# A block-sparse attention and feed-forward kernel on one core: block table by two VectorE operations, opening loads reordered, issue times of the DMA queue in the scheduler

## The chip, the core and the metric

The kernel runs on one NeuronCore of a Trainium2 chip. The metric is the device time of one execution in microseconds (us), the median of several. The engines are TensorE (PE in the profile; PEld is its weight load), VectorE (DVE), ScalarE (ACT), GpSimd (POOL) and SyncE (SP), which here only issues transfers. A DMA can be issued by SP, ACT or POOL, each with its own queue.

Runs more than 1.5% above the fastest of the same kernel count as slow; ratios use fast runs alone. A span (first to last instruction) is a little shorter than the time of the same run (275.8 and 277.58 us in the profiled run of the changed kernel).

## The reference, cut to what matters

```python
q, k, v: (4, 8, 768, 64)   sampled_blocks: (24, 3)   w_in: (512, 2048)   w_out: (2048, 512)
mask = |blk_i - blk_j| <= 1, or first/last block row or column, or kb in sampled_blocks[qb]   # blocks of 32
attn = softmax(where(mask, q @ k.T / 8, -1e9)) @ v
x    = attn.transpose(0, 2, 1, 3).reshape(4 * 768, 512)
out  = relu(x @ w_in) ** 2 @ w_out
```

## The kernel before

Heads go in pairs: `u` is a head pair, 0 to 3 in the first image, 4 to 15 in the other three. Scores are made transposed (keys by queries), go through one exponential per tile on ACT (`pT`), are multiplied on DVE by a table of the mask (`MK`), and meet the values on PE. The result, normalized (`xq`), is transposed (`xT`) by PE in the first image and by a transposing DMA in the others, and goes through the two layers (`ph` is the hidden one, `py` the output). PE must do all matmuls, so the kernel is built to keep PE fed.

The first 256 queries need the mask before `MK` exists. They get it by an extra matmul of a block table `oh` (128x768, one where a key lies in a block) with mask rows `R`. `oh` was cut out by GpSimd, and copied to the other half by DVE:

```python
V.memset(oh, 1.0)
G.affine_select(out=o3, in_=o3, compare_op=AOP.is_ge, fill=0.0, base=0, ...)
G.affine_select(out=o3, in_=o3, compare_op=AOP.is_ge, fill=0.0, base=block - 1, ...)
V.tensor_copy(out=oh[D:P, :], in_=oh[0:D, :])
```

The loads of the opening are a list: queue, head pair, which of queries 0, keys 1, values 2, and which part. Rows are 1536 bytes for a whole load, 768 for half of the keys, 512 for the first two of six query chunks:

```python
sy.dma_start(out=sb_i, in_=sampled_blocks.bitcast(I32))
for eng, u, w, ns in ((sc_, 0, 1, KEYS[0]), (sy, 0, 0, QRS[0]), (sc_, 1, 1, ALL), (sy, 0, 1, KEYS[1]),
                      (sy, 1, 0, QRS[0]), (sy, 0, 2, ALL), (sc_, 1, 2, ALL), (sy, 2, 1, ALL),
                      (sy, 2, 0, QRS[0]), ...
```

Everything after that is placed by a list scheduler in the program itself. It keeps a modelled clock per engine, takes the task that can start first (or an urgent one), and so fixes the order in which each engine gets its instructions. It never sees the chip: it works from numbers such as these.

```python
LAT = {"PE": 0.23, "DVE": 0.06, "ACT": 0.06, "POOL": 0.08, "SP": 2.0}
LEAD = 13.709                                 # how far ahead casts of later keys may start
arrive = {(0, 1, 0): 4.15, (0, 0, 0): 4.7, (0, 1, CP): 6.4, (0, 2, 0): 8.8, (1, 1, 0): 7.0, ...   # opening loads
ld_t = T_(("SP", 1.3), s0 - 30, load, u, (sy, sy, sy), ..., dma=3.3)             # loads of u >= 4
mu[u, q0] = T_(("SP", 0.5), s - 9, x_transp_dma, u, q0, w, deps=[nm], ..., dma=0.4)
```

The softmax here doesn't subtract the row's maximum and nothing guards it: scores larger than these inputs give would overflow.

## Time and profile before

| | before |
|---|---|
| time, median of 3 | 280.29 us (279.68 to 281.26) |
| span of the profiled run | 279.2 us |
| PE / ACT / DVE / POOL busy | 96% / 73% / 70% / 38% |
| PE waits for `xT` | once, 3.0 us, near 104 us |

How to read it: PE is the bound, so each microsecond is either PE's work or PE's lost time. The stretches of the profile show where it is lost. Columns are the window, its length, busy time and count of PE, weight load, DVE, ACT and POOL, then the granted clock, the DMA share and GB/s.

```profile
0.00:31.00 31.00, 27.50 (x468) 20.82 (x470) 24.63 (x71) 21.42 (x32) 14.62 (x33) 1.00 1.05 248
...
101.00:109.00 8.00, 4.97 (x38) 2.40 (x33) 2.96 (x7) 3.27 (x6) 2.01 (x3) 0.79 1.04 219
```

PE lacks 3.5 of 31 us in the opening and 3.0 of 8 us where the second image's hidden layer starts. In that second stretch the clock too falls to a mean of 0.79. In the opening, the timeline (start, duration, engine, line, operation, out<-in, and in brackets the idle time before it and what ended it) shows what the first tiles hang on.

```profile
1.79 0.51 ACTq L221 DMA_DIRECT2D vs<-in_v_dram  x1
...
6.37 0.23 PE L386 MATMUL ps<-QK 64*128 64x128 bf16 x2
...
7.01 0.81 ACT L397 ACTIVATE pT<-ps 128x768 bf16<-128x768 f32 x1 [1.57 <-PE ps L390]
7.17 1.02 DVE L195 CAST qc<-ks 128x384 bf16<-128x384 f32 x2 [0.71 <-DMA ks<-in_k_dram]
...
7.78 0.34 PE L338 MATMUL pt<-identb,qc 128*128 128x128 bf16 x3 [0.81 <-DVE qc L195]
```

The first score tile starts at 6.37, its exponential at 7.01, and the second half of the first keys is cast at 7.17. ACT's queue takes 384 KB of values (pair 1) at 1.79 us, among the first loads.

### The profile page before, as it was taken

Reading aid. Unit: us, or ns where it says so; the run is one execution under the profiler, and the core shown is the slowest. Engines: PE = TensorE matmul, PEld = TensorE weight load, DVE = VectorE, ACT = ScalarE, POOL = GpSimd, SP = SyncE. Lnnn points to the kernel's source line nnn. Section 1 sums busy time; section 2 is a strip of 40 time slices with the busy share of each in tenths; the row PEclk is TensorE's granted clock in tenths of the full one; section 3 lists DMA queues with packets and bytes.
Section 4 is the critical chain, followed back from the end, with each engine's and each line's share of the span. In section 5 each row is a group of like instructions: output and inputs, shape, how many; then the busy total and the mean of one; then the engine's idle time right before and its main releaser. Section 6 shows DMA issues by size and latency. Waiting matters only on the chain.

```text
span 279.2 us, 7467 instructions
## 1 busy us (share of the span) xinstructions
PE 268.4 (96%) x3037; PEld 164.1 (59%) x3037; DVE 195.7 (70%) x394; ACT 202.4 (73%) x304; POOL 107.1 (38%) x136
## 2 busy tenths in 40 slices
PE   8889999999999969999999999999999999999995
PEld 5668767566766535566555565555555555555544
DVE  7877899899687836778867688676767774344400
ACT  3588989899999765999899798978988850011111
POOL 4462437564756314444312132111131426655500
PEclk9999999999999997999999999999999999999999
DMA  6999999999915997462033344212101111111112
GB/s 217 366 231 206 197 236 368 316 340 278 255 22 90 258 246 248 59 197 59 12 72 80 86 116 52 65 21 59 47 13 56 40 32 47 39 40 38 38 67 85
DMA packets 51882, 36.93 MB, mean 132 GB/s; under 512 B 30984, under 2 KB 48904, under 8 KB 51848
## 3 DMA queue, kind: packets, MB, share of 16 engines
q1 hardware_dynamic: 46808, 31.27, 41.5%
q0 software_dynamic: 4224, 4.19, 9.3%
q10 hardware_dynamic: 816, 0.98, 1.0%
q8 instruction: 24, 0.39, 0.6%
q14 instruction: 10, 0.08, 0.1%
HBM read 27.26 MB, written 6.29 MB: 120 GB/s over the span
## 4 chain that ended last, share of the span: by engine, by line
PE 83%; DMA 7%; DVE 6%; ACT 2%; issue 1%; SPq 1%; ACTq 0%; DVEq 0%
PE ph L473 28%; PE py L514 28%; PE po L419 13%; PE ps L386 12%; DVE pT L404 3%; DMA qs<-in_q_dram 3%; DMA vs<-in_v_dram 2%; DMA xT<-xq 2%; DVE qc L195 1%; ACT pT L397 1%; PE pk L308 1%; DVE xq L429 1%; PE po L436 1%; PE ps L390 0%; SPq L221 0%
## 5 line engine op out<-in xcount | busy, mean ns | idle before, releaser
L397 ACT ACTIVATE pT<-ps 128x1024 bf16<-128x1024 f32 (+1 forms) x148 | 140.3, 1000 | 14.2 <-PE ps L386 8.9
L491 POOL TENSOR_TENSOR g<-r 128x384 bf16<-128x384 f32 (+1 forms) x86 | 75.1, 876 | 130.5 <-DVE r L482 71.9
L473 PE MATMUL ph<-xT,w_in_sb 128*128 128x384 bf16 (+2 forms) x640 | 108.1, 296 | 3.0 <-DMA xT<-xq 3.0
L404 DVE TENSOR_TENSOR pT<-pT,MK 128x1024 bf16<-128x1024 bf16 x132 | 101.4, 784 | 10.9 <-ACT pT L397 10.5
L514 PE MATMUL py<-w_out_sb,g 128*128 128x512 bf16 (+1 forms) x400 | 102.3, 370 | 0.1
L473 PEld LDWEIGHTS <-w_in_sb 128*128 128x128 bf16 x640 | 52.8, 98 | 33.2 <-issue 4.4
L482 DVE TENSOR_SCALAR r<-ph 128x384 f32<-128x384 f32 (+1 forms) x82 | 43.1, 527 | 38.3 <-PE ph L473 30.8
L419 PEld LDWEIGHTS <-pT 128*128 128x128 bf16 x1152 | 47.3, 98 | 21.2 <-issue 5.1
L419 PE MATMUL po<-VT,pT 128*128 128x65 bf16 x1152 | 54.6, 194 | 0.4 <-DVE xT L195 0.3
L514 PEld LDWEIGHTS <-g 128*128 128x128 bf16 x400 | 36.0, 97 | 25.5 <-issue 1.5
L386 PE MATMUL ps<-QK 64*128 64x256 bf16 (+1 forms) x624 | 47.6, 263 | 0.4 <-ACT pT L397 0.2
L489 ACT ACTIVATE g<-r 128x384 bf16<-128x384 f32 (+1 forms) x58 | 28.7, 496 | 19.1 <-DVE r L482 18.3
L386 PEld LDWEIGHTS <-QK 64*128 64x128 bf16 x624 | 25.1, 94 | 22.5 <-issue 18.8
L193 ACT COPY ys<-py 128x512 f32<-128x512 f32 (+1 forms) x23 | 13.0, 567 | 31.8 <-PE py L514 31.7
L480 ACT ACTIVATE r<-ph 128x256 f32<-128x256 f32 (+1 forms) x62 | 26.3, 444 | 4.7 <-PE ph L473 3.7
L195 POOL CAST VT<-vs 128x768 bf16<-128x768 f32 x15 | 13.9, 932 | 25.2 <-PE po L419 16.5
L429 DVE TENSOR_TENSOR xq<-po,rs 128x256 bf16<-128x256 f32 (+1 forms) x52 | 21.0, 404 | 1.8
L427 DVE RECIPROCAL rs<-po 128x4 f32<-128x4 f32 (+1 forms) x52 | 9.1, 175 | 13.6 <-PE po L419 13.4
L195 DVE CAST qc<-qs 128x768 bf16<-128x768 f32 (+2 forms) x14 | 8.8, 632 | 0.9 <-DMA qs<-in_q_dram 0.9
L195 DVE CAST qc<-ks 128x768 bf16<-128x768 f32 (+1 forms) x11 | 7.8, 713 | 1.2 <-DMA ks<-in_k_dram 1.2
L390 PE MATMUL ps<-R,oh 64*128 64x128 bf16 x96 | 6.8, 216 | 0.0
L338 PE MATMUL pt<-identb,qc 128*128 128x128 bf16 x48 | 4.9, 226 | 1.8 <-DVE qc L195 1.8
(55 smaller groups left out, 74.6 us busy)
## 6 DMA issues: line engine op xcount, KB each, us to landing
out_dram<-ys SPq DMA_DIRECT2D x23, 256.0 KB, 2.0
vs<-in_v_dram SPq DMA_DIRECT2D x15, 384.0 KB, 6.0
ks<-in_k_dram SPq DMA_DIRECT2D x14, 384.0 KB, 5.1
qs<-in_q_dram SPq DMA_DIRECT2D x12, 384.0 KB, 4.2
w_in_sb<-in_moe_w_in_dram POOLq DMA_DIRECT2D x4, 512.0 KB, 9.3
w_out_sb<-in_moe_w_out_dram POOLq DMA_DIRECT2D x4, 512.0 KB, 12.1
qs<-in_q_dram SPq DMA_DIRECT2D x4, 256.0 KB, 7.1
xT<-xq SPq DMA_TRANSPOSE x36, 2.3
```

Of the source, the lines that this page charges most:

```text
L195: (V if e == "DVE" else G).tensor_copy(out=out, in_=in_)
L386: nc.tensor.matmul(ps[:, h, j * w:(j + 1) * w], QK[i][hs, 1, ksl], QK[i][hs, 0, qsl], start=j == 0, stop=not add, skip_group_check=True)
L397: A.activation(out=pT[:, :, 0:n], in_=stile.pop(a)[:, :, 0:n], func=AF.Exp, scale=scale)
L404: V.tensor_tensor(out=pT, in0=pT, in1=m[:, None].broadcast_to([P, 2, len(cs), w]), op=AOP.mult)
L419: nc.tensor.matmul(po[:, qc, h, :], pT[:, h, j * w + qc * P:j * w + (qc + 1) * P], VT[i][:, h, n, 0:VW], start=(n == 0 and qc == 0 and h = ...
L429: V.tensor_tensor(out=xq, in0=po[:, :, :, 0:D], in1=rs.broadcast_to([P, n, 2, D]), op=AOP.mult)
L473: nc.tensor.matmul(htile[T, f][:, i * w:(i + 1) * w], w_in_sb[:, kc, f_ * P:(f_ + 1) * P], xT[b][:, kc, c0:c0 + w], start=(kc == 0), stop= ...
L480: A.activation(out=r, in_=src, func=AF.Relu)
L482: V.tensor_scalar(out=r, in0=src, scalar1=0.0, scalar2=None, op0=AOP.max)
L489: A.activation(out=g, in_=r, func=AF.Square)
L491: (G if e == "POOL" else V).tensor_mul(out=g, in0=r, in1=r)
L514: nc.tensor.matmul(ytile[T, i], gtile[T, f][:, ts * P:(ts + 1) * P], w_out_sb[:, f, cs[0]:cs[1]], start=(f == 0), stop=(f == NF - 1))
```

## The change

Its intent: free GpSimd and VectorE in the opening by a cheaper block table, load in the order of need, and give the scheduler truer times for SP's DMA queue, so that loads no longer stand in front of an urgent transpose. Constants of the scheduler were tuned again around it. The core of the diff:

```diff
-    N_WARM, N_IDLE = 15, 24
+    N_WARM, N_IDLE = 14, 24
-    MASKED = ((256, 768, 17.0), (0, 256, 38.0))
+    MASKED = ((256, 512, 12.0), (512, 768, 20.0), (0, 256, 38.0))
-    LAT = {..., "SP": 2.0}
+    LAT = {..., "SP": 1.4}
-    LEAD = 13.709
+    LEAD = 9.283
...
-    sy.dma_start(out=sb_i, in_=sampled_blocks.bitcast(I32))
-    for eng, u, w, ns in ((sc_, 0, 1, KEYS[0]), (sy, 0, 0, QRS[0]), (sc_, 1, 1, ALL), (sy, 0, 1, KEYS[1]),
-                          (sy, 1, 0, QRS[0]), (sy, 0, 2, ALL), (sc_, 1, 2, ALL), (sy, 2, 1, ALL),
-                          (sy, 2, 0, QRS[0]), (sy, 3, 1, ALL), (sy, 3, 0, QRS[0]), (sy, 2, 2, ALL), (sy, 3, 2, ALL),
+    for eng, u, w, ns in ((sc_, 0, 1, KEYS[0]), (sy, 0, 0, QRS[0]), (sc_, 1, 1, ALL), (sy, None, 0, ALL), (sy, 0, 1, KEYS[1]),
+                          (sy, 1, 0, QRS[0]), (None, 0, 0, ALL), (sc_, 0, 2, ALL), (sy, 2, 1, ALL), (sy, 2, 0, QRS[0]),
+                          (sy, 3, 1, ALL), (sy, 3, 0, QRS[0]), (sy, 1, 2, ALL), (sy, 2, 2, ALL), (sy, 3, 2, ALL),
...                       # u None: the block list; eng None: the load of ACT's function table
-    V.memset(oh, 1.0)
-    G.affine_select(out=o3, ...)          # twice
-    V.tensor_copy(out=oh[D:P, :], in_=oh[0:D, :])
+    V.tensor_scalar(out=place.rearrange("a (j i) -> a j i", i=block), in0=blk[:, 0:nb, None].broadcast_to([P, nb, block]),
+                    scalar1=blk[:, nb:nb + 1], scalar2=None, op0=AOP.is_equal)
+    V.tensor_copy(out=oh.rearrange("a (n p) -> a n p", p=P), in_=place.rearrange("a (p n) -> a n p", n=NCH))
...
-    arrive = {(0, 1, 0): 4.15, (0, 0, 0): 4.7, (0, 1, CP): 6.4, (0, 2, 0): 8.8, (1, 1, 0): 7.0, (1, 0, 0): 7.4, ...
+    arrive = {(0, 1, 0): 3.7, (0, 0, 0): 3.8, (0, 1, CP): 5.0, (1, 0, 0): 5.7, (1, 1, 0): 5.8, (0, 2, 0): 7.8, ...
-            ld_t = T_(("SP", 1.3), ..., dma=3.3)
+            ld_t = T_(("SP", 1.6), ..., dma=4.0)
-                    mu[u, q0] = T_(("SP", 0.5), ..., dma=0.4, **kw)
+                    mu[u, q0] = T_(("SP", 1.22), ..., dma=0.6, **kw)
...                       # likewise the transposes of later keys and queries, the stores, the relu and
...                       # square biases (0.364, 0.372 -> 0.192, 0.21), PACE, AHEAD, TIES and the start times
```

More of the change, by code (lines that the diff above doesn't have):

```diff
@@ L77 @@
     QT0, ADDED, ALONE = [(0, 128), (128, 128), (256, 256), (512, 256)], (0, 128), (0, 128)
-    MASKED = ((256, 768, 17.0), (0, 256, 38.0))
+    MASKED = ((256, 512, 12.0), (512, 768, 20.0), (0, 256, 38.0))
     tasks = []
-    LAT = {"PE": 0.23, "DVE": 0.06, "ACT": 0.06, "POOL": 0.08, "SP": 2.0}
+    LAT = {"PE": 0.23, "DVE": 0.06, "ACT": 0.06, "POOL": 0.08, "SP": 1.4}
     OVER = {"PE": 0.0, "DVE": 0.08, "ACT": 0.09, "POOL": 0.03, "SP": 0.0}
     SWITCH, SHARE, SLACK = 0.096, 0.85, 0.1
-    AHEAD = {"PE": 0.007, "DVE": 0.022, "ACT": 0.153, "POOL": 0.0, "SP": 0.0}
-    LEAD = 13.709
-    PACE0, PACE, SINGLE, MASK_AT = 39.252, 1.548, 1, 17.0
+    AHEAD = {"PE": 0.027, "DVE": 0, "ACT": 0.139, "POOL": 0.0, "SP": 0.0}
+    LEAD = 9.283
+    PACE0, PACE, SINGLE, MASK_AT = 43.821, 1.719, 1, 17.0
     class Buf:
@@ L89, in __init__ @@
             self.pool, self.holds, self.free = pool, 0, 0.0
-    TIES = 369548, 1.681, 1.912
+    TIES = 808178, 1.778, 0.874
     def tie(n):
@@ L225 @@
     sb_i = consts.tile([nb, n_rand * 2], I32, name="sb_i")
-    sy.dma_start(out=sb_i, in_=sampled_blocks.bitcast(I32))
-    for eng, u, w, ns in ((sc_, 0, 1, KEYS[0]), (sy, 0, 0, QRS[0]), (sc_, 1, 1, ALL), (sy, 0, 1, KEYS[1]),
-                          (sy, 1, 0, QRS[0]), (sy, 0, 2, ALL), (sc_, 1, 2, ALL), (sy, 2, 1, ALL),
-                          (sy, 2, 0, QRS[0]), (sy, 3, 1, ALL), (sy, 3, 0, QRS[0]), (sy, 2, 2, ALL), (sy, 3, 2, ALL),
+    for eng, u, w, ns in ((sc_, 0, 1, KEYS[0]), (sy, 0, 0, QRS[0]), (sc_, 1, 1, ALL), (sy, None, 0, ALL), (sy, 0, 1, KEYS[1]),
+                          (sy, 1, 0, QRS[0]), (None, 0, 0, ALL), (sc_, 0, 2, ALL), (sy, 2, 1, ALL), (sy, 2, 0, QRS[0]),
+                          (sy, 3, 1, ALL), (sy, 3, 0, QRS[0]), (sy, 1, 2, ALL), (sy, 2, 2, ALL), (sy, 3, 2, ALL),
                           (sy, 0, 0, QRS[1]), (sy, 1, 0, QRS[1]), (sy, 2, 0, QRS[1]), (sy, 3, 0, QRS[1])):
-        load_part(eng, u, w, ns)
-    nc.scalar.add_instruction(mybir.InstLoadActFuncSet(
-        act_func_set_id=ACT_SET_LN_EXP, name=nc.get_next_instruction_name(),
-        engine=mybir.EngineType.Activation, ins=[], outs=[]))
+        if eng is None:
+            nc.scalar.add_instruction(mybir.InstLoadActFuncSet(
+                act_func_set_id=ACT_SET_LN_EXP, name=nc.get_next_instruction_name(),
+                engine=mybir.EngineType.Activation, ins=[], outs=[]))
+        elif u is None:
+            sy.dma_start(out=sb_i, in_=sampled_blocks.bitcast(I32))
+        else:
+            load_part(eng, u, w, ns)
     warm = consts.tile([P, 256], BF, name="warm")
@@ L241 @@
     oh = consts.tile([P, S], BF, name="oh")
-    V.memset(oh, 1.0)
     bm = consts.tile([nb, P], BF, name="bm")
     V.memset(bm, 0.0)
+    place = consts.tile([P, S], BF, name="place")
+    blk = consts.tile([P, nb + 1], F32, name="blk")
     junk = ps_h.tile([P, 512], F32, name="junk", tag="h")
@@ L250 @@
     rel = consts.tile([nb, nb], F32, name="rel")
-    col = consts.tile([nb, nb], F32, name="col")
-    row = consts.tile([nb, 1], F32, name="row")
     small = dict(allow_small_or_imprecise_dtypes=True)
+    G.iota(blk[:, 0:nb], pattern=[[1, nb]], base=0, channel_multiplier=0, **small)
+    for h in range(2):
+        G.iota(blk[h * D:(h + 1) * D, nb:nb + 1], pattern=[[0, 1]], base=0, channel_multiplier=1, **small)
     G.iota(rel, pattern=[[1, nb]], base=0, channel_multiplier=-1, **small)
-    G.iota(col, pattern=[[1, nb]], base=0, channel_multiplier=0, **small)
-    G.iota(row, pattern=[[0, 1]], base=0, channel_multiplier=1, **small)
+    col, row = blk[0:nb, 0:nb], blk[0:nb, nb:nb + 1]
     identb = consts.tile([P, P], BF, name="identb")
     make_identity(nc, identb)
-    o3 = oh.rearrange("a (n p) -> a n p", p=P)
-    G.affine_select(out=o3, in_=o3, compare_op=AOP.is_ge, fill=0.0, base=0,
-                    pattern=[[1, NCH], [NCH, P]], channel_multiplier=-block)
-    G.affine_select(out=o3, in_=o3, compare_op=AOP.is_ge, fill=0.0, base=block - 1,
-                    pattern=[[-1, NCH], [-NCH, P]], channel_multiplier=block)
     QK, VT = [], []
@@ L528, in T_ @@
         return Task(engs, key, (lambda e: f(*args, e)), **kw)
-    arrive = {(0, 1, 0): 4.15, (0, 0, 0): 4.7, (0, 1, CP): 6.4, (0, 2, 0): 8.8, (1, 1, 0): 7.0, (1, 0, 0): 7.4, (1, 2, 0): 9.1,
-              (2, 1, 0): 9.8, (2, 0, 0): 9.9, (3, 1, 0): 11.4, (3, 0, 0): 11.7, (2, 2, 0): 12.8, (3, 2, 0): 13.8}
-    arrive.update({(u, 0, 2): (14.6, 16.2, 16.6, 17.3)[u] for u in range(HP)})
+    arrive = {(0, 1, 0): 3.7, (0, 0, 0): 3.8, (0, 1, CP): 5.0, (1, 0, 0): 5.7, (1, 1, 0): 5.8, (0, 2, 0): 7.8, (2, 1, 0): 7.9, (2, 0, 0): 8.3,
+              (3, 1, 0): 9.4, (3, 0, 0): 9.8, (1, 2, 0): 10.8, (2, 2, 0): 11.9, (3, 2, 0): 12.95}
+    arrive.update({(u, 0, 2): (14.9, 15.4, 16.1, 16.8)[u] for u in range(HP)})
     KEYS_OF = {P: [tuple(range(CP)), tuple(range(CP, NCH))], QW: [(2 * c, 2 * c + 1) for c in range(CP)]}
@@ L554, in prepare @@
             g = gate[GATES[min(u - HP, len(GATES) - 1)]]
-            ld_t = T_(("SP", 1.3), s0 - 30, load, u, (sy, sy, sy),
-                      deps=cv[u - NRAW] + tr[u - NRAW] + [g], dma=3.3)
+            ld_t = T_(("SP", 1.6), s0 - 30, load, u, (sy, sy, sy),
+                      deps=cv[u - NRAW] + tr[u - NRAW] + [g], dma=4.0)
             at = dict(deps=[ld_t])
@@ L562, in prepare @@
                 tr[u].append(c)
-                x = T_(("SP", 1.0), s0 - 10, transp_dma, u, w, deps=[c] + old_s, put=[qc], dma=1.2)
+                x = T_(("SP", 1.25), s0 - 10, transp_dma, u, w, deps=[c] + old_s, put=[qc], dma=1.5)
                 ev[u].update({(w, n): x for n in range(NCH)})
@@ L575, in prepare @@
                 opts["ACT"] = 0.23 + 0.1 * n
-                if u or (w == 0 and ns.start):
+                if u or w == 0:
                     opts["POOL"] = 0.1 + 0.15 * n
@@ L588, in prepare @@
             for i in range(2 * NWP):
-                wl[i] = T_(("POOL", 0.85), -50 + i, w_load, i, after=12.9 + 2.55 * i - (1.7 if i else 0), late=1.3, dma=2.55)
+                wl[i] = T_(("POOL", 0.85), -50 + i, w_load, i, after=11.9 + 2.6 * i - (1.7 if i else 0), late=1.3, dma=2.62)
             for i in GATES:
@@ L613, in attend @@
                 ob[u, q0] = Buf("po")
-            va = T_(("PE", 0.245 * part), s + 2.929, values, a, deps=[ex] + cv[u] + va_all[-1:],
+            va = T_(("PE", 0.245 * part), s + 2.393, values, a, deps=[ex] + cv[u] + va_all[-1:],
                     get=[] if cs[0] else [ob[u, q0]], put=[pt], mode=128)
@@ L627, in attend @@
                 if by_dma:
-                    mu[u, q0] = T_(("SP", 0.5), s - 9, x_transp_dma, u, q0, w, deps=[nm], put=[xqb], dma=0.4, **kw)
+                    mu[u, q0] = T_(("SP", 1.22), s - 9, x_transp_dma, u, q0, w, deps=[nm], put=[xqb], dma=0.6, **kw)
                     continue
@@ L639 @@
         rb_ = Buf("ps")
-        t = T_(("PE", 0.11 + 0.11 * i), -90 + i, mask_rows, c0, c1, after=9.5 if i else 5.5, get=[rb_], put=[], mode=32)
-        mr.append(T_({"ACT": 0.4 + 0.2 * i, "DVE": 0.3 + 0.2 * i}, -88 + i, mask_rows_evac, c0, c1, deps=[t], put=[rb_], after=10.0 if i else 0.0))
+        t = T_(("PE", 0.11 + 0.11 * i), -90 + i, mask_rows, c0, c1, after=8.5 if i else 4.15, get=[rb_], put=[], mode=32)
+        mr.append(T_({"ACT": 0.4 + 0.2 * i, "DVE": 0.42 + 0.25 * i}, -88 + i, mask_rows_evac, c0, c1, deps=[t], put=[rb_], after=8.5 if i else 0.0))
     for i in range(N_IDLE):
@@ L693 @@
                         put=[xb[b]] if last_use else [], mode=128)
-                rr = T_(RELU[w], 200, relu, t, f, deps=[h1], get=[rb], put=[hb], bias={"ACT": 0.364})
-                sq = T_(SQ[w], n_key, square, t, f, deps=[rr], get=[gb], put=[rb], bias={"ACT": 0.372})
+                rr = T_(RELU[w], 200, relu, t, f, deps=[h1], get=[rb], put=[hb], bias={"ACT": 0.192})
+                sq = T_(SQ[w], n_key, square, t, f, deps=[rr], get=[gb], put=[rb], bias={"ACT": 0.21})
                 sq_of.update({(t, f + i): sq for i in range(per_unit(t))})
@@ L711 @@
                     yc = T_({"ACT": 0.22 + 0.365 * n, "DVE": 0.15 + 0.53 * n}, 150, out_copy, t, i, cs, deps=[yy], get=[sb], put=[yb])
-                    T_(("SP", 0.2), 0, store, t, i, ts, cs, deps=[yc], put=[sb], late=2.0)
-    run_schedule({"PE": 4.65, "DVE": 5.3, "ACT": 4.15, "POOL": 4.4, "SP": 16.0},
+                    T_(("SP", 0.55), 0, store, t, i, ts, cs, deps=[yc], put=[sb], late=2.0, dma=0.7)
+    run_schedule({"PE": 4.2, "DVE": 4.0, "ACT": 3.65, "POOL": 3.7, "SP": 16.0},
                  {"ps": 2, "po": 1, "h": 2, "y": 1, "pT": PT_BUFS, "r": R_BUFS, "g": G_BUFS, "ys": YS_BUFS,
-                  "qc": QC_BUFS, "xq": XQ_BUFS, "xT": XT_BUFS}, dma_free=16.4)
+                  "qc": QC_BUFS, "xq": XQ_BUFS, "xT": XT_BUFS}, dma_free=15.4)
 _INS = ['q', 'k', 'v', 'sampled_blocks', 'moe_w_in', 'moe_w_out']
```

## The prediction

> **What bounds the kernel now.** First I read the page's busy times, to see which engine the end can hang on:
>
> ```profile
> PE 268.4 (96%) x3037; PEld 164.1 (59%) x3037; DVE 195.7 (70%) x394; ACT 202.4 (73%) x304; POOL 107.1 (38%) x136
> ```
>
> TensorE (PE) is busy for 96% of 279.2 us, so time can only come from its idle stretches and from matmuls that run slower than they must. "Busy" hides the second kind, so I made a ledger: every matmul in program order, priced at the start-to-start time that the chain of waits shows for an undisturbed run of its form (eight 256-wide hidden matmuls in 0.87 us, so 0.109 each; four 384-wide in 0.65; four 512-wide output ones in 0.86; sixteen value ones in 0.59; eight 256-wide score ones in 0.54; 128-wide score pairs 0.056 a pair). The sum is 260.6 us. Setting it against the true start of each matmul shows where the other 18.6 us go:
>
> - 1.3 before the first matmul;
> - 7.0 between there and 31 us (the opening);
> - 1.7 from 31 to 101 us;
> - 4.7 from 101 to 109 us;
> - 0.3 in the following 167 us;
> - 3.6 from the last matmul's start to the end (last copy and store).
>
> Two of these are what the change can reach. Next I asked the chain of waits about the 4.7 us; columns are start, duration, what:
>
> ```profile
> 99.57 5.36 DMA xT<-xq
> 104.97 1.78 PE ph L473 x5
> ```
>
> A transposing DMA of x, issued at 99.57, holds the first hidden matmuls of batch 1. The DMA queue's timeline shows why it came so late: its xq was written by 96.65, but the queue was first busy with three loads (0.58 + 0.46 + 0.47 us of issuing), another transpose (1.17) and a store:
>
> ```profile
> 95.99 0.58 SPq L210 DMA_DIRECT2D qs<-in_q_dram  x1
> 96.62 0.46 SPq L210 DMA_DIRECT2D ks<-in_k_dram  x1
> 97.12 0.47 SPq L210 DMA_DIRECT2D vs<-in_v_dram  x1
> 97.69 1.17 SPq L448 DMA_TRANSPOSE xT<-xq  x1
> 98.96 0.52 SPq L523 DMA_DIRECT2D out_dram<-ys  x1
> 99.57 1.19 SPq L448 DMA_TRANSPOSE xT<-xq  x1
> ```
>
> Then it took 5.36 us to land, behind those loads' 1.2 MB, where the median transpose lands in 2.3. The stretches of one microsecond show the price; columns are PE, weight load, DVE, ACT, POOL busy, then the granted clock, DMA share, GB/s:
>
> ```profile
> 103.00:104.00 1.00, 0.00 (x0) 0.00 (x0) 0.00 (x0) 0.33 (x1) 0.00 (x0) 1.00 0.86 130
> 104.00:105.00 1.00, 0.03 (x1) 0.03 (x2) 0.00 (x0) 0.00 (x0) 0.00 (x0) 0.77 1.14 279
> 105.00:106.00 1.00, 1.00 (x4) 0.50 (x5) 0.41 (x1) 0.00 (x0) 0.00 (x0) 0.50 1.14 323
> ```
>
> PE stands still for 3.03 us, and as it resumes the granted clock is 0.50 for some 3 us more: the five matmuls of the chain took 1.78 us instead of 5 x 0.162 = 0.8. Ledger: 3.2 of standing, 1.5 of half clock.
>
> Last, the opening, in the timeline:
>
> ```profile
> 2.14 0.83 DVE L277 SCALAR_TENSOR_TENSOR pm<-rel,pm 24x24 f32<-24x24 f32 x1
> 3.01 1.25 DVE L279 TENSOR_SCALAR al<-pm,edge 24x24 f32<-24x24 f32 x1
> 9.47 0.81 ACT L397 ACTIVATE pT<-ps 128x768 bf16<-128x768 f32 x1 [1.65 <-PE ps L390]
> 15.85 0.74 DVE L195 CAST qc<-qs 128x512 bf16<-128x512 f32 x1 [0.91 <-DMA qs<-in_q_dram]
> ```
>
> Two 24x24 operations take 0.83 and 1.25 us while GpSimd runs the two affine selects of the block table; bm is ready at 5.57. ACT, which must do 16 exponentials before the wide tiles start, has its second only at 9.47 because keys of head pair 0 (second half) were cast at 7.17; the late queries at 15.85 then hold PE for 1.1 us. DMA moved 362 GB/s from 5 to 8 us, so the opening is a matter of which bytes come first.
>
> **What the Trainium skill says.** "TensorE: Matmul & The Clock Gate", What's actually happening: an idle window of about 3.4 us sends TensorE to half clock and about 3.4 us of activity brings it back, the window running freely. The trace agrees (3.03 us idle, then 0.50), so a wait of 3 us costs half as much again and a wait of 0.5 us should cost itself alone. "GPSIMD Engine Reference", Specifications: GpSimd shares SBUF interfaces with VectorE, in contention with VectorE's 2-port modes and two-input operations. Agrees: 0.83 and 1.25 us beside the affine selects, 0.10 to 0.13 us for their neighbours of the same size. "DMA: Bandwidth & Descriptors", Issuing engines are not separate DMA queues: issuing on several engines saves only the sequencer's time. So moving loads between ACT's and SP's queues gains order, not bandwidth.
>
> **The change part by part.** *Block table.* Out: memset (0.70), two affine selects on POOL (0.87, 0.86), copy of half (0.35). In: one tensor_scalar and one strided copy of 128x768 on DVE. I put them at 0.4 to 0.9 us each (the memset of that shape takes 0.70), the same DVE time, but 2 us of POOL work go and the two slowed operations should shrink by about 1.8 us together. bm at about 4.4, 1.2 us earlier. POOL being free also takes the first query cast.
>
> *Loads.* The first query load is issued at once rather than behind the block list (0.50 us earlier), and the 384 KB of values of pair 1 move behind the keys of pairs 2 and 3. At 362 GB/s that is 1.1 us that all data in between come earlier. The second exponential should start near 8 us instead of 9.5, the fifth near 12 instead of 13.6; the late queries can gain no more than the 0.5 us of the earlier start. They held PE before; in the new order PE meets their transposes about 1 us of work later, so that wait should mostly go. Sum: the wide tiles (exponential 17, at 26.0 before) start about 1.5 us earlier. These gains are on the path, as PE's order is fixed and everything behind shifts.
>
> *Queue model.* No instruction changes, but the order does. I counted, in the two programs, PE work between the last value matmuls that a hidden tile needs and its first hidden matmul. For the stalled tile it is 5.41 us before and 4.15 after, so less. But in the new queue order that transpose has a store and a transpose in front, and no loads nearby. It then needs 0.7 (reciprocal 0.18, multiply 0.42, semaphores), 0.1 for the queue, and 2.3 to land, 3.1 in all: under 4.15. At the other batch changes the program leaves 4.58 us twice, and 4.55 sufficed at one of them before. So I take 4.4 of the 4.7 us as gained.
>
> *Mask table in two steps.* 18 mask matmuls of 256 instead of 6 of 512 and 6 of 256: equal columns on PE, six more evacuations, each 0.1 to 0.2 us of overhead: about 1 us spread over ACT and DVE.
>
> *Engine choice.* The lower bias sends squares to ACT: 58 to 89, and relus 62 to 72, off POOL and DVE. Back to back these cost ACT 0.26 to 0.43 us, so some 13 us more, of which 15 squares fall after the last scores where ACT idles. But between exponentials 20 and 56 my sum of ACT's work rises from 48.6 to 51 us, against PE work of 51.2: ACT is then as full as PE. I charge 0.4 us there and 0.2 later.
>
> *PE work itself*: one warm-up matmul less, 0.2.
>
> Sum: -1.5 -4.4 -0.2 +0.4 +0.2 = -5.5, at most. Some of the opening's gain will meet the weight loads, which run at full DMA rate from 14 to 37 us and begin only about 0.5 to 1 us earlier: I take back 0.4. So 280.3 - 5.1 = 275.2.
>
> **The rivals.**
> 1. *The stall stays or moves.* Only 4.15 us lie in front of the first hidden matmul, and DVE could be inside a mask product (0.68 us, up to 1.4 in this trace) when the values end. For it: the margin is one microsecond, and the last of four accumulation steps adds 0.5. Against: the freed queue. A wait of 1 us would give 276.2; the full stall with its half clock 279.8.
> 2. *ACT becomes the bound from 31 to 100 us.* For it: its sum equals PE's. If every extra microsecond of ACT's work showed up, the 2.4 us would give 277.2. Against: from exponential 80 to 92 ACT was busy 17.3 of 18.7 us and PE lost nothing.
> 3. *The opening gains nothing*, because DMA carries the same bytes and the late queries still arrive near 15.5. Then 276.7. Its opposite, all gaps of ACT before 25 us (4.7 us in sum) halved, gives 274.
>
> **Range and chances.** Removing the stall is the solid part (4 to 5 us), the opening 0.5 to 2.3, ACT's price 0 to 2. So 275.2, with 273.5 to 277.8 for 8 in 10. Faster by over 2% needs 274.7, just below my number: 0.41; within 2%: 0.58; slower by over 2% would need a new stall of twice the old one: 0.01.
>
> **What would show each step.** The chain should have no piece of several us of the x transpose near 100 us, and no stretch with PEclk below 0.9 after the warm-up; that transpose should be issued within 0.2 us of its xq and land in about 2.3. The two 24x24 operations should take under 0.3 us, bm be ready before 4.8, the second exponential start before 8.5 and the seventeenth near 24.5. ACT's idle time between 31 and 100 us should shrink without PE waiting on "pT" or "ps" for more than 2.5 us in sum. The prediction is wrong if PE shows a wait of over 1 us after 30 us, or if the seventeenth exponential starts after 25.5.

## The result, and the profile after

The changed kernel takes 277.23 us (median of 4, 276.86 to 278.12) against 280.12 for before. The ratio is 0.9895 with a 95% interval of 0.9855 to 0.9935, a gain of 1.05%. A ratio is the mean time of one kernel's fast runs over that of the other's of the same rounds, so it is not quite the ratio of the medians quoted beside it. The point prediction was 275.2; the range held, the sum did not.

The page's busy times and clock row, after (the clock in tenths, 40 slices):

```profile
PE 266.1 (96%) x3003; PEld 165.4 (60%) x3042; DVE 192.1 (70%) x389; ACT 219.4 (80%) x349; POOL 74.4 (27%) x101
...
PEclk9689999999999999999999999999999999999999
```

ACT has more to do, POOL less, as intended. (39 matmul records are missing, so x3003; all weight loads are there.) The low digits of the clock row have moved from the 16th slice to the second: out of the image change, into the opening. The stretches:

```profile
0.00:31.00 31.00, 26.85 (x433) 20.20 (x434) 21.45 (x65) 20.39 (x34) 11.77 (x31) 0.89 1.06 248
31.00:101.00 70.00, 69.06 (x931) 47.65 (x944) 58.38 (x120) 65.18 (x111) 23.93 (x31) 1.00 0.84 204
101.00:109.00 8.00, 7.95 (x88) 4.56 (x88) 6.64 (x12) 7.37 (x14) 4.63 (x6) 1.00 0.90 207
```

From 101 to 109 us PE is now busy for 7.95 of 8.00 us at full clock (4.97 and 0.79 before). In the opening it does less than before, at 0.89 of the clock. SP's queue shows how the stall went:

```profile
95.27 1.17 SPq L448 DMA_TRANSPOSE xT<-xq  x1
96.62 0.45 SPq L523 DMA_DIRECT2D out_dram<-ys  x1
98.38 1.18 SPq L448 DMA_TRANSPOSE xT<-xq  x1
```

No load stands between them. The normalized tile is written at 98.34 and its transpose is issued at 98.38, lands 2.3 us later, near 100.7, and the first hidden matmul starts at 101.67 with PE never idle.

The opening is the other half. The chain of waits of the changed kernel (start, duration, what):

```profile
2.21 6.02 DMA qs<-in_q_dram
8.25 0.83 DVE qc L195
9.13 0.40 PE pt L338 x2
```

The load of 128 KB of queries for pair 1, issued at 2.21, takes 6.02 us. The timeline beside it, with VectorE's part first:

```profile
1.29 0.73 DVE L269 TENSOR_SCALAR place<-blk 128x768 bf16<-128x768 f32 x1
2.06 0.94 DVE L271 COPY oh<-place 128x768 bf16<-128x768 bf16 x1
...
3.32 0.28 DVE L280 TENSOR_SCALAR al<-pm,edge 24x24 f32<-24x24 f32 x1
...
4.71 0.18 DVE L288 TENSOR_SCALAR bm<-pm 24x48 bf16<-24x48 f32 x1
...
6.87 0.55 DVE L195 CAST qc<-ks 128x384 bf16<-128x384 f32 x1 [1.08 <-DMA ks<-in_k_dram]
```

The block table does what it should: the 24x24 operation that took 1.25 us takes 0.28, and `bm` is ready at 4.89 instead of 5.57. But VectorE then stands idle for 1.08 us until the second half of the first keys lands. The rest of the timeline:

```profile
1.83 0.46 ACTq L221 DMA_DIRECT2D vs<-in_v_dram  x1
...
7.48 0.34 PE L338 MATMUL pt<-identb,qc 128*128 128x128 bf16 x3 [1.46 <-DVE qc L195]
...
8.30 0.81 ACT L397 ACTIVATE pT<-ps 128x768 bf16<-128x768 f32 x1
...
11.11 0.61 PE L322 MATMUL idle<-warm 128*128 128x128 bf16 x4
11.21 0.81 ACT L397 ACTIVATE pT<-ps 128x768 bf16<-128x768 f32 x1 [2.10 <-PE ps L390]
```

In this order PE meets the transposes of that key half *before* the first scores, so the first exponential starts at 8.30 instead of 7.01 and the second at 11.21 instead of 9.47. The line of `idle` matmuls is a useful clock: these keep-warm matmuls never change, and four of them in a row take 0.61 us here, at half clock, and 0.40 at full clock (shown for another run below). ACTq's line explains the load: the values of pair 0, formerly on SP's queue, are now on ACT's at 1.83, where those of pair 1 were at 1.79 before. ACT's queue carries as many bytes in the first microseconds as it did before.

The prediction's ledger can be made for every trace: the start of each weight load minus the undisturbed cost of all PE work in front of it is the time lost so far. By stage, in us ("opening" is up to 22.5 us of PE work, near 30 us; "image change" from 90 to 95 us of work, near 100; the tail runs from the last weight load to the end):

| profiled run | opening | middle | image change | later | tail | PE work | span |
|---|---|---|---|---|---|---|---|
| before | 8.07 | 1.63 | 4.81 | 0.36 | 3.8 | 260.6 | 279.2 |
| changed | 10.51 | 0.67 | 0.23 | 0.45 | 3.7 | 260.4 | 275.8 |
| changed, run again | 8.93 | 0.69 | 0.23 | 0.45 | 3.6 | 260.4 | 274.2 |

(The last matmul's own work, about 0.1 us, lies in the tail, so the sums run 0.1 over.) The stall is gone, 4.6 us. The middle gains 1.0. The opening gives 2.4 us back in one profiled run and 0.9 in another of the same kernel.

### The profile page after: what moved, and what is told of

It is laid out like the page before. It is cut to its first block, busy times and chain, and to the rows that moved or that the text cites.

```text
span 275.8 us, 7401 instructions
## 1 busy us (share of the span) xinstructions
PE 266.1 (96%) x3003; PEld 165.4 (60%) x3042; DVE 192.1 (70%) x389; ACT 219.4 (80%) x349; POOL 74.4 (27%) x101
## 4 chain that ended last, share of the span: by engine, by line
PE 88%; ACT 4%; DMA 2%; DVE 2%; issue 1%; SPq 0%; ACTq 0%
PE py L514 28%; PE ph L473 28%; PE po L419 14%; PE ps L386 13%; ACT pT L397 3%; DMA qs<-in_q_dram 2%; PE pt L338 1%; PE ps L390 1%; PE pk L308 1%; DVE pT L404 1%; PE idle L322 1%; DVE qc L195 1%; ACT r L480 1%; ACT g L489 1%; PE po L436 1%
## 5 line engine op out<-in xcount | busy, mean ns | idle before, releaser
L404 DVE TENSOR_TENSOR pT<-pT,MK 128x1024 bf16<-128x1024 bf16 x132 | 100.1, 775 | 11.9 <-ACT pT L397 11.3
L473 PE MATMUL ph<-xT,w_in_sb 128*128 128x384 bf16 (+2 forms) x640 | 105.7, 294 | 0.1
L514 PE MATMUL py<-w_out_sb,g 128*128 128x512 bf16 (+1 forms) x361 | 94.4, 370 | 1.8
L491 POOL TENSOR_TENSOR g<-r 128x384 bf16<-128x384 f32 (+1 forms) x55 | 48.6, 889 | 167.3 <-ACT r L480 87.3
L482 DVE TENSOR_SCALAR r<-ph 128x384 f32<-128x384 f32 (+1 forms) x72 | 36.7, 512 | 29.7 <-PE ph L473 28.7
L489 ACT ACTIVATE g<-r 128x384 bf16<-128x384 f32 (+1 forms) x89 | 43.2, 494 | 17.7 <-DVE r L482 17.1
L480 ACT ACTIVATE r<-ph 128x384 f32<-128x384 f32 (+1 forms) x72 | 31.9, 464 | 6.2 <-PE ph L473 5.9
L193 ACT COPY ys<-py 128x512 f32<-128x512 f32 (+1 forms) x19 | 10.7, 565 | 10.2 <-PE py L514 10.2
L195 DVE CAST qc<-ks 128x768 bf16<-128x768 f32 (+1 forms) x13 | 10.1, 774 | 1.1 <-DMA ks<-in_k_dram 1.1
L390 PE MATMUL ps<-R,oh 64*128 64x128 bf16 x96 | 7.7, 231 | 0.0
```

What stands on the lines that cost most here:

```text
L195: (V if e == "DVE" else G).tensor_copy(out=out, in_=in_)
L404: V.tensor_tensor(out=pT, in0=pT, in1=m[:, None].broadcast_to([P, 2, len(cs), w]), op=AOP.mult)
L473: nc.tensor.matmul(htile[T, f][:, i * w:(i + 1) * w], w_in_sb[:, kc, f_ * P:(f_ + 1) * P], xT[b][:, kc, c0:c0 + w], start=(kc == 0), stop= ...
L480: A.activation(out=r, in_=src, func=AF.Relu)
L482: V.tensor_scalar(out=r, in0=src, scalar1=0.0, scalar2=None, op0=AOP.max)
L489: A.activation(out=g, in_=r, func=AF.Square)
```

## The experiments

My theory after the result had two parts. First, the stall went because no loads stand in front of the transpose, whichever number of the scheduler moved them. Second, the opening got slower because PE's new order is written for loads that arrive near 5.0 and 5.7 us (the new `arrive` table), while ACT's queue still takes the bandwidth with values that nobody needs yet. Rivals: the block table is the cause, the mean clock of the opening is an accident of these runs, or the retuned order alone is slower. Twelve kernels ran; before had medians of 279.25, 279.95 and 279.92 us (11 runs each). All results were correct.

### The changed kernel again

No edit.

> The changed kernel again, beside the others of this call. Theory: 277.2 us; the first exponential near 8.3 and the second near 11.2 us, later than the 7.0 and 9.5 of the kernel before, in every run and not only in the profiled one. Rival: the slow opening belongs to that one profiled execution, whose granted clock fell to 0.5 from 8.4 to 15.3 us; then the second exponential comes before 9.5 us here and the time goes under 276.

Measured: 278.33 us (276.01 to 280.23), ratio 0.9938 [0.9886, 0.9990]; one of the six runs is slow. In the profiled run, the fastest of the six, the first two exponentials start at 8.13 and 10.45 us, late as expected; the other runs have no trace. The spread of 4 us is wider than that of any variant below in which the second exponential starts before 10 us (at most 2.4), but the kernel before, whose second starts at 9.47, spreads by 3.2 to 6.0 us over its 11 runs, so spread alone does not point to late keys. The gain over before lies between 0.6% (here) and 1.05%.

### Values of pair 0 behind the first keys and queries

```diff
-  (sy, 1, 0, QRS[0]), (None, 0, 0, ALL), (sc_, 0, 2, ALL), ...
+  (sy, 1, 0, QRS[0]), (None, 0, 0, ALL), (sy, 0, 2, ALL), ...
```

All orders on PE, DVE, ACT and POOL are those of the changed kernel; one load changes its queue.

> The changed kernel with one load moved: the values of head pair 0 go from ACT's queue to SP's, behind the first queries of pair 1. All five engines' compute orders are the same. Theory (the 384 KB on ACT's queue take turns with the keys and queries on SP's queue and delay them): the second half of the keys of pair 0 is cast before 5.8 us (6.87 now), the queries of pair 1 before 6.5 (8.25 now), the second exponential starts before 8.6 (11.21 now), the granted clock stays at 1.0 after the warm-up, and the time falls by 1.5 to 2.5 us to about 275.2. Rival (SP's small rows are slow by themselves, whatever ACT's queue does): these loads land at most 0.3 us earlier and the time stays at 277.

Measured: 274.87 us (273.57 to 275.98), ratio 0.9824 [0.9784, 0.9863], against 0.9938 for the changed kernel. The timeline:

```profile
5.66 0.55 DVE L195 CAST qc<-ks 128x384 bf16<-128x384 f32 x1
6.40 0.29 DVE L195 CAST qc<-qs 128x256 bf16<-128x256 f32 x1 [0.18 <-DMA qs<-in_q_dram]
...
8.10 0.40 PE L322 MATMUL idle<-warm 128*128 128x128 bf16 x4
8.21 0.81 ACT L397 ACTIVATE pT<-ps 128x768 bf16<-128x768 f32 x1 [0.30 <-PE ps L390]
```

The keys are cast at 5.66 (6.87 in the changed kernel), the queries at 6.40 (8.25), the second exponential starts at 8.21 (11.21), and the keep-warm matmuls run at full clock. The bytes that landed on each queue in each microsecond, counted from the transfer records, in KB:

```
us from start          2-3  3-4  4-5  5-6  6-7
changed     ACT queue   99  359  154  210   97
            SP queue   108    4  175   47  216
values late ACT queue   90  362  123    0    0
            SP queue   109    5  219  281  376
```

From 3 to 4 us nearly everything goes to ACT's queue in both (359 and 362 KB against 4 and 5). This is no sharing yet: by the transfer records SP's queue had only the block list (24 rows of 24 bytes) and the last few query rows to move then, and its half of the keys, issued at 1.77 and 1.75, began at 4.11 and 4.15. After that the changed kernel still gives ACT's queue 461 KB to 7 us, mostly values, where this one gives SP's queue, with the key half and the queries at its head, 876 KB. So the second part of the theory holds: one load in the wrong place in the queues costs some 3 us. Part of that goes with the clock (see the ledgers at the end). This is also a version that beats both kernels.

### The old block table

```diff
+    V.memset(oh, 1.0)                      # and the two affine_selects, and the copy of half,
-    V.tensor_scalar(out=place...)          # exactly as in the kernel before
-    V.tensor_copy(out=oh..., in_=place...)
```

This was made twice: from the changed kernel, and from the one with the values late.

> The changed kernel with the block table made the old way (memset, two affine selects, copy), all else as it is; PE's and ACT's orders are the same. Theory (the table is off the path, since the first scores wait for the keys' second half at 7.75 us): the mask rows' operand bm is ready some 0.6 us later, and the time stays within 0.4 us of the changed kernel's. Rival (bm is on the path): slower by 0.7 us or more.

> The version with the values of pair 0 behind pair 1's queries, with the block table made the old way. Theory: bm comes 0.5 us later (5.35 instead of 4.85), but the first scores still wait for the keys at about 6.6, so the time is within 0.4 us of that version's 274.9. Rival (now that the keys come earlier bm is on the path): 0.5 us or more slower.

Measured: 279.11 us, ratio 0.9964 [0.9921, 1.0007], in the first case; 275.46 us, ratio 0.9826 [0.9785, 0.9868], in the second. By medians both tests came out for the rival (0.78 us slower against a threshold of 0.7, 0.59 against 0.5). But the second pair ran in two calls, and before was 0.7 us slower in the later one; against 0.9938 and 0.9824 with the new table, the ratios differ by 0.0026 and 0.0002, and the intervals overlap widely. `bm` starts at 5.17 in both with the old table, 4.71 with the new. So no gain of the block table can be told from the scatter, and the opening's loss is not its doing. With the affine selects back, the two 24x24 operations take 0.83 and 0.89 us again (0.16 and 0.28 without them), so the old table is what slows them; the 1.25 us in the trace of before was a single draw.

### The stall alone, taken away by moving three loads

In the kernel before, the three loads of one head pair (13) are kept back until two more transposes of x have been issued. Nothing else changes order on any engine.

```diff
+    DEFER = 13
+        if u == DEFER:
+            late.append((load_now, (u, engs)))      # emitted behind the 2nd next transpose of x
```

> The kernel before with the three loads of one later head pair issued behind the next two transposes of x instead of in front of them; nothing else moves on any engine. Theory (the loads' issue time and bytes in front of the transpose made the stall): the transpose is issued within 0.3 us of its xq near 96.7, lands in 2.3 us, PE has no wait near 101 us and no half clock, and 4.7 us go: 275.6. Rival 1 (the transpose lands late for other reasons, such as the transposes of keys and queries around it): a wait of 1.5 us or more stays and the time is above 278. Rival 2 (the loads, now later, hold up something else): the wait goes but the time falls by less than 3 us.

Measured: 275.82 us (275.48 to 277.43), ratio 0.9879 [0.9838, 0.9921]. SP's queue:

```profile
97.31 1.19 SPq L457 DMA_TRANSPOSE xT<-xq  x1
98.55 0.57 SPq L219 DMA_DIRECT2D qs<-in_q_dram  x1
```

The transpose is issued at 97.31 (99.57 in before), the loads follow it, and the ledger's image change falls from 4.81 to 0.18 us. So this one move gains 3.4 us, no less than the whole change does. The first part of the theory holds, but for one detail: the transpose goes out 1.1 us after its `xq` (written at 96.18), not within 0.3, since another transpose and a store still stand in front.

### The old load order in the changed kernel

```diff
+  (sy, 1, 0, QRS[0]), (sy, 0, 2, ALL), (sc_, 1, 2, ALL), (sy, 2, 1, ALL), ...    # list and table load as before
-  (sy, 1, 0, QRS[0]), (None, 0, 0, ALL), (sc_, 0, 2, ALL), (sy, 2, 1, ALL), ...
```

> The changed kernel with the loads of the opening issued in the order of the kernel before (and the activation table loaded after them); PE's, DVE's and GpSimd's orders stay. Theory (the new order of loads gave the keys' second half and pair 1's queries nearly nothing, since ACT's queue still carries 384 KB of values beside them; what made the opening slow is that PE's new order puts the first scores behind those keys): the first exponential stays at 8 us or later, and the time is within 0.7 us of the changed kernel's 278.3. Rival (the new order of loads is worth the 1.1 us that I predicted): slower by 1 us or more, with the second half of the keys over 1 us later.

Measured: 276.68 us (275.44 to 278.34), ratio 0.9884 [0.9837, 0.9931]. With the new order on PE but the old loads, the first two exponentials start at 8.97 and 10.90, about as late as in the changed kernel (8.30, 11.21), and the second half of the keys is cast at 7.07 (6.87). The median is 1.6 us lower, outside the 0.7 that I allowed, though the intervals overlap. So the reordering of the loads gained nothing that can be seen in this kernel: in both, PE's order asks early for keys that neither load order brings early.

### The queue's issue times, alone and taken out

Alone, put into the kernel before:

```diff
-    LAT = {..., "SP": 2.0}          # loads 1.3/3.3, transposes 1.0/1.2 and 0.5/0.4, store 0.2
+    LAT = {..., "SP": 1.4}          # loads 1.6/4.0, transposes 1.25/1.5 and 1.22/0.6, store 0.55/0.7
```

Taken out: the reverse edit in the changed kernel.

> The kernel before with only the modelled issue times, landing times and latency of the DMA queue of the change (load, two kinds of transposes, store). Theory (those numbers did not remove the stall: in this program a loads' triple still stands three places in front of the transpose that batch 1 waits for, with 3.99 us of PE work behind the values): a wait of PE for the transpose of x of 2 us or more near 100 us, and a time of 279 to 281. Rival (the modelled times are what removed it): no wait over 0.5 us there and a time under 276.5.

> The changed kernel with the old issue times, landing times and latency of the DMA queue; pacing, lead, ties and biases stay new. Theory (pacing and lead moved the loads away from the transpose, not the issue times): no PE wait over 0.5 us for a transpose of x at the first tile of batch 1, although 4.15 us of PE work lie in front of it; the time is within 1.5 us of the changed kernel's, either way. At batch 2 and 3 only 3.6 and 3.8 us are left, so waits of up to 0.5 us may show. Rival (the issue times matter): a stall of 2 us or more with half clock, and 280 or more.

Measured: alone 279.78 us, ratio 0.9983 [0.9936, 1.0031]; taken out 279.97 us, ratio 0.9967 [0.9914, 1.0019]. Neither profile has a wait of PE for `xT`, so the wait of 2 us that I expected with the times alone did not come. The place lost 2.45 us there all the same, for another reason:

```profile
101.01 0.42 PE L419 MATMUL po<-VT,pT 128*128 128x65 bf16 x8 [1.28 <-DVE pT L404]
```

PE waited 1.28 us for a mask product on VectorE. So the new issue times are not sufficient: they moved the stall to another operand. With the times taken out, the image change costs nothing (0.02), so they are not necessary for it either. That run lost in the opening (11.85) and the middle (2.08) instead. Among the eight profiled runs of the changed kernel and its variants with two mask steps, the four whose opening lost 11.0 us or more lost 0.97 to 2.08 in the middle, the four others 0.67 to 0.84 (see the ledgers at the end). In these four the full clock came for good only at 16.9 us or later (see there). Whether the issue times or the late start cost the 1.4 us there is left open.

### The pacing alone

```diff
-    LEAD = 13.709
+    LEAD = 9.283
```

This goes into the kernel before and is the smallest edit of all.

> The kernel before with one number changed, the lead of the scheduler's pacing (LEAD, from its old value to that of the change); issue times, block table, mask table and opening are those of before. In the order that results the loads of the later head pair stand five places or more ahead of the transposes that stalled. Theory (what ends the stall is where those loads stand, whichever number moves them): no wait of over 1 us for xT, and 276 to 277.5. Rival (the issue times of the queue are needed for it): a wait of 2 us or more stays at the start of the second image, 279 or more.

Measured: 276.59 us (275.94 to 277.95), ratio 0.9913 [0.9866, 0.9959]. No wait for `xT`; the transpose goes out at 97.84 and the nearest loads at 99.08, behind it. The theory held, the rival (2 us or more stay) fell: one number, with no issue time touched, moves the loads. The image change still loses 0.83, and the ratio is not to be told from that of the deliberate move of the three loads (0.9879).

### Extra keep-warm matmuls in the opening

```diff
+        for _ in range(12 if (u, w, ns.start) == (0, 1, CP) else 0):
+            keep_warm(e)
```

> The changed kernel with 12 further keep-warm matmuls (128 columns, results never read) on TensorE just before the transposes of the second half of the first keys; the order of everything else is the same on every engine. Theory (part of the changed kernel's loss is the clock: while TensorE idles for late loads in the opening, the full clock comes late or is lost again): the profile shows the full clock before 10 us and no half clock after it until the first score tiles are through; the first exponential is not earlier than 8.1 us, and the median falls by about 1 us against the changed kernel, to 276.3 to 277.3. Rival (the clock of the opening does not matter, because TensorE waits for data there anyway): the same 277 to 278, or up to 0.7 us longer for the added matmuls.

Measured: 276.43 us (275.10 to 280.50), ratio 0.9887 [0.9833, 0.9941] from the four fast runs of six; the profiled run is slow (280.5 us). The median lies in the expected range, but the interval overlaps that of the changed kernel (0.9938), so the gain is not settled; and the profile contradicts the mechanism:

```profile
5.68 2.23 PE L322 MATMUL idle<-warm 128*128 128x128 bf16 x19
8.21 0.50 PE L340 MATMUL pt<-identb,qc 128*128 128x128 bf16 x3 [0.30 <-DVE qc L195]
...
11.74 0.61 PE L322 MATMUL idle<-warm 128*128 128x128 bf16 x4
```

Nineteen keep-warm matmuls fill PE from 5.68 to 7.9 us at 0.11 us each, against 0.06 in the run with the values late (2.23 and 0.40 us, less the last one's own 0.3 or 0.2, by the number of intervals). Four at 11.74 still take 0.61, although no wait since 4.9 was longer than 0.3 us. The expected full clock before 10 us did not come, so filling the idle time does not secure it. The runs fall into two groups, 275.1 to 276.5 and 279.5 to 280.5; that these are openings at full and at half clock is possible but not shown, as only one trace exists. What stays unproven is that filling the idle time brings the full clock; what the half clock costs is worked out at the end.

### Both causes mended in the kernel before

The loads of pair 13 are kept back as above, and the values of pair 1 leave ACT's queue:

```diff
-  (sy, 0, 2, ALL), (sc_, 1, 2, ALL), (sy, 2, 1, ALL), ..., (sy, 3, 0, QRS[0]), (sy, 2, 2, ALL), ...
+  (sy, 0, 2, ALL), (sy, 2, 1, ALL), ..., (sy, 3, 0, QRS[0]), (sy, 1, 2, ALL), (sy, 2, 2, ALL), ...
```

> The kernel before with two changes of the load queues alone: the three loads of the one later head pair are put behind the next two transposes (as in the run with the loads behind), and the values of the second pair go to SyncE's queue behind the third pair's queries, instead of ScalarE's queue at the start. All orders on TensorE, VectorE, ScalarE and GpSimd are those of before. Theory (the values on ScalarE's queue take bandwidth from the keys and queries in their first microseconds in either kernel): the opening gains about 1 us on top of what the loads behind gave, 274.3 to 275.3, and the second exponential starts before 9.0 us (9.47 before). Rival (in the order of before the keys and queries are early enough and the values cost nothing): 275.5 to 276, as with the loads behind alone.

Measured: 275.83 us (275.24 to 277.43), ratio 0.9879 [0.9832, 0.9927], the same as with the loads behind alone (0.9879). The second exponential starts at 8.93, as the theory said, but the time is the rival's. The chain shows where it went:

```profile
6.62 8.87 DMA vs<-in_v_dram
15.51 0.56 DVE VT L196
```

Values now come late: their load is issued at 6.62, they are cast at 15.51 (14.2 with the loads behind alone), and PE waits 1.24 us until 16.54 for what VectorE does next. In this order of PE, which expects values early, earlier keys gained nothing. The gain of late values is thus that of an order and a load list that fit each other, not of the load list alone.

### The mask table in one step again, with the values late

```diff
-    MASKED = ((256, 512, 12.0), (512, 768, 20.0), (0, 256, 38.0))
+    MASKED = ((256, 768, 17.0), (0, 256, 38.0))
```

> The changed kernel with the values of the first pair on SyncE's queue (as in the run with the values late), and the mask table for 256 to 768 made in one step again, as before; the scheduler places a few later pieces otherwise. Theory (the two steps only spread work of ScalarE and VectorE that is not on the path): within 0.8 us of the run with the values late, 274.1 to 275.7. Rival (the two steps are part of the gain of the stretch from 31 to 101 us): 276 or more.

Measured: 275.90 us (275.62 to 276.54), ratio 0.9884 [0.9843, 0.9924], against 0.9824 with two steps. By ratio that is 0.6%, 1.7 us, with intervals that overlap; the median lies between the two expectations. The ledger loses 7.84 in the opening (6.34) and 1.22 in the middle (0.84). So the two steps, which I had priced as a small cost, may be part of the gain, but the scheduler placed other pieces differently too, and neither the cause nor the size is settled.

### All ledgers

Time lost by stage in the profiled run, and the results:

| run | opening | middle | image change | later | median us | ratio |
|---|---|---|---|---|---|---|
| changed, again | 8.93 | 0.69 | 0.23 | 0.45 | 278.33 | 0.9938 |
| values late | 6.34 | 0.84 | 0.23 | 0.45 | 274.87 | 0.9824 |
| old table | 11.67 | 1.82 | 0.23 | 0.45 | 279.11 | 0.9964 |
| before, loads behind | 7.50 | 1.74 | 0.18 | 0.36 | 275.82 | 0.9879 |
| old load order | 11.00 | 0.97 | 0.23 | 0.45 | 276.68 | 0.9884 |
| before, issue times | 7.35 | 1.61 | 2.45 | 1.30 | 279.78 | 0.9983 |
| without issue times | 11.85 | 2.08 | 0.02 | 0.88 | 279.97 | 0.9967 |
| values late, old table | 7.63 | 0.67 | 0.23 | 0.45 | 275.46 | 0.9826 |
| keep-warm (slow run) | 11.00 | 1.90 | 0.71 | 0.53 | 276.43 | 0.9887 |
| before, both mended | 8.61 | 1.41 | 0.20 | 0.36 | 275.83 | 0.9879 |
| before, new LEAD | 7.60 | 1.34 | 0.83 | 0.33 | 276.59 | 0.9913 |
| values late, one step | 7.84 | 1.22 | 0.18 | 0.77 | 275.90 | 0.9884 |

A profiled run is one draw, and the opening scatters from draw to draw (10.51 and 8.93 for the same kernel); the ledgers only say where. Nor are the draws alike: of its six runs the profiled one is the fastest for "changed, again", "values late", "before, issue times", "values late, old table" and "before, new LEAD", and the slowest for "old table", "old load order", "without issue times", "keep-warm" and "before, both mended".

Much of the opening's loss and of its scatter goes with the clock. A trace's clock records begin when the full clock first comes: four keep-warm matmuls take 0.61 us at 10.80 in the run with the old load order (first record at 16.90), and 0.40 at 10.34 in the changed kernel run again (first record at 10.26). By these records:

| runs | full clock for the rest of the opening from | extra time of PE work at half clock before that |
|---|---|---|
| before and its variants | 5.2 to 7.2 us | 0.5 to 1.3 us |
| changed; run again | 15.3; 10.3 | 3.0; 2.2 |
| old table, old load order, without issue times, keep-warm | 16.9 to 18.0 | 4.4 to 5.4 |
| values late; with one step; with old table | 4.6; 4.7; 9.0 | 0; 0; 1.7 |

The last column is an estimate: the ledger's price of every matmul that starts before the full clock (the warm-up matmuls left out), since a matmul at half clock takes about that much longer (keep-warm ones 0.11 us each instead of 0.06). Taken off the opening's loss it leaves 7.6 us for before, 7.5 and 6.8 for the changed kernel and 6.3 for values late. So in the ledger the changed opening is longer not by more waiting but by work at half clock. This books the time; it does not say what a full clock would have gained, since PE might then have waited longer for data. Where the full clock had come by 5.1 us, it was lost near 8 us in the three runs with the values on ACT's queue, where PE's longest waits were 0.98 to 1.61 us, and kept in the two with the values late, whose waits were 0.54 us at most. In the other runs with PE's new order it had not come by then, and why is not shown.

## Why the prediction was right or wrong

**What bounds the kernel: right.** PE stayed the bound: 260.4 of the 275.8 us are its undisturbed work, and the two stretches named are where the time moved.

**The stall: right in mechanism and size.** Predicted -4.4; the ledger's image change went from 4.81 to 0.23, -4.6. One reading was loose. I let 3.03 us of idle time agree with the 3.4 us of the page that I cited, but the clock record falls at 104.54, 2.6 us after PE's last matmul ended (101.94), and in the changed kernel's opening it fell at 8.43 with no wait longer than 1.46 us before it. So a short wait does not always cost itself alone, as I had concluded. The order did leave the time that I had counted: needed 3.1 of 4.15 us, and the transpose landed about 1 us before its first matmul. Rival 1 (the stall stays or moves) did not come true in the changed kernel, though it did in the run with the issue times alone. What I called the queue model's work is not the issue times' alone: the pacing number by itself also moves the loads.

**Loads: the step that failed.** I wrote that "the 384 KB of values of pair 1 move behind the keys of pairs 2 and 3", and that all data in between come 1.1 us earlier, worth -1.5. I read what left the early queue and not what took its place: the values of pair 0, just as large, stand in ACT's queue where those of pair 1 stood. The queries of pair 1 landed near 8.23, and the second half of the first keys was cast at 6.87, 0.3 earlier instead of 1.1. Meanwhile the scheduler's arrival table says 5.7 and 5.0, and PE's order was built on that. The second exponential was to start near 8 and started at 11.21 and 10.45 in two profiled runs; the seventeenth near 24.5, and it started at 28.19 and 26.61. The term was -1.5 and measured +2.4 and +0.9; by the estimate above, work at half clock (3.0 and 2.2 us against 0.5 in before) accounts for all of it, a cost that the prediction did not have. The late queries' wait did go (0.95 us before, none after). The prediction's own test ("after 25.5" is wrong) failed, and so did its sign that no stretch after the warm-up would fall below 0.9 of the clock (0.50 from 8.43 to 15.26). That the total still lay near the forecast is partly luck: the middle gained 1.0 us where I had charged 0.4. Putting that one load where I thought it was gave 24.01 for the seventeenth exponential, 8.21 for the second, and 274.87 us for the whole, close to the 275.2 predicted; how much of that is earlier keys and how much the earlier clock is not separated.

I had cited the Trainium skill, "DMA: Bandwidth & Descriptors", Issuing engines are not separate DMA queues, for several issuers saving only the time of issuing. The same page, Queues, rings and completion order, says that each DMA engine takes turns between queues packet by packet. I had drawn "order, not bandwidth" from the first and missed what the second implies: bytes on a second queue are not behind those on the first. From 4 to 6 us, when both queues had rows waiting, the trace is in line with that: 330 rows (227 KB) started on SP's queue and 234 (351 KB) on ACT's.

**Block table: nearly right, but off the path.** 0.73 and 0.94 us against 0.4 to 0.9; the slowed pair of 24x24 operations went from 2.08 to 0.44 us (predicted to shrink by 1.8, shrank by 1.6). Of the neighbours that I called the same size, only one is 24x24 (0.10 us), the others 24x1. `bm` was ready at 4.89, where I said 4.4, and before 4.8 as a sign. Its undoing moved the times by less than the intervals.

**Engine choice and mask table: wrong in sign.** I charged 0.4 us from 31 to 100 us. ACT's busy time there did rise (63.60 to 65.18 us), but PE lost 0.67 instead of 1.63. Rival 2, ACT as the bound, is refuted. The cause of the gain is not fully settled; the run with one mask step leaves the two steps possible for part of it.

**PE work: right** (260.6 to 260.4). **Later and tail:** +0.2 predicted; +0.09 and -0.16 measured. The 0.4 that I took back for the weight loads can't be told apart from the rest of the opening.

Put together for the profiled pair: +2.44 - 0.96 - 4.58 + 0.09 - 0.20 - 0.16 = -3.37, and the spans are 279.2 and 275.8. The number of rival 2, 277.2, is the median of 277.23 by luck, since its mechanism is refuted; rival 3, an opening that gains nothing, named 276.7 and is nearer in kind, but the opening lost.

## What to carry to other kernels

When loads are reordered, list what stands on each queue at each microsecond before and after; a large load that leaves an early place has gained nothing if an equally large one that nobody needs yet moves in. A static order and its table of arrival times belong together: measure arrivals and put them into the table, since an engine with a fixed order waits for the one late operand with everything behind it. And before crediting a remodelled scheduler, try the shortest edit that removes the stall seen in the trace; here moving three loads gave 3.4 us, as much as the whole change.

## What the Trainium skill lacked or had wrong

- "DMA: Bandwidth & Descriptors", Queues, rings and completion order: turns between queues are stated, but not what share of the bytes each gets. Here it went by rows rather than bytes: from 5 to 6 us the kernel before started 155 rows on SP's queue (116 KB, nearly all of 768 bytes) and 153 on ACT's (230 KB, of 1536). From 4 to 5 us it was 105 against 183, so the turns were not always even. Why is not shown.
- "TensorE: Matmul & The Clock Gate", What's actually happening: about 3.4 us of sustained activity is said to bring the full clock, the moment varying by half a microsecond either way. In the run with the old load order, PE had no wait over 0.2 us from 7.67 us on, four keep-warm matmuls still took 0.61 us (half clock) at 10.80, and the full clock came at 16.90. In the slow run with extra keep-warm matmuls the same holds from 9.77 us on, and it came at 17.06. Page and measurement differ; the measurement stands. Why it came so late is not shown.
- That the clock records of a trace may begin late stands on no page; the one on TensorE says only that they can be unreliable. The profile page of the keep-warm run prints full clock in every slice, while the durations of its matmuls (0.61 us for four, 0.40 at full clock) say otherwise up to its first record at 17.06.
